# Second-layer expert weights in half-expert parts with two rows a partition: attention and soft mixture of experts on one core

## The chip, the cores and the metric

The kernel runs on 1 core of one Trainium2 chip. The metric is the device time of one execution in microseconds. A core has five engines with queues of their own: TensorE (PE for its matmuls, PEld for its weight loads), VectorE (DVE), ScalarE (ACT), GpSimd (POOL) and SyncE (SP). Transfers are issued from the queues of POOL (these can change the type on the way, here float32 to bfloat16) and of SP (no change of type), and are carried by the same 16 transfer engines.

## The reference

```
q, k, v: (8, 12, 448, 64)         # batch, heads, sequence, head width
scores = 30 * tanh(q @ k.T / sqrt(64) / 30)
attn   = exp(scores - max) / sum
x      = (attn @ v), heads side by side -> (3584, 768)

logits = x @ phi                                  # 3584 x 32: 8 experts x 4 slots
d = softmax of logits over the 3584 tokens;   slot_input = d.T @ x          # 32 x 768
h = relu(slot_input[e] @ w1[e]);   slot_out[e] = h @ w2[e]                  # w1 768x1024, w2 1024x768
c = softmax of logits over the 32 slots;      out = c @ slot_out            # 3584 x 768, float32
```

All eight experts' weights are read once: w1 and w2 are 25 MB each in float32, and no more than 4 rows (slots) pass through each expert.

## The kernel before, in words

**Attention** takes the first 234 us. Heads are worked in pairs, 48 of them; scores of three key tiles at a time go from TensorE (`qk_chunk`, L432) through ScalarE's tanh (`tanh_chunk`, L442) into tiles of six, and then through exp, on ScalarE (`exp_part`, L446) for some tiles and as a polynomial on VectorE (`poly_exp`, L466 to L474, with scratch tiles xf and xp) for the others. TensorE multiplies by v (`pv_mms`, L495), VectorE normalises (L507), and logits and slot sums follow a batch at a time.

**The order is written out by hand** in the string `PROGRAM` (L196 to L243), one letter per step, and each engine does its share in that order. T is a tanh step (0 to 111), Q its scores, E and p the two kinds of exp, A and B the product with v, J and K the transposition of a raw q or k (L389); the transposition of one quad of heads issues the load of the quad after next into the same place (`load`, L278, on POOL's queue). G, N and F are filler matmuls without a use of their own. **M n issues the n-th weight cast** (`wjobs`, L138 to L154), also on POOL's queue.

**The weight casts.** 16 of w1, half an expert each, straight into SBUF (L129). w2 is cut into 64 blocks of 128 rows, ordered so that four experts stand side by side, and four blocks make a part (16 parts, 768 KB each in bfloat16). SBUF has no room for all of w2 during the attention, so most of it is *spilled*: cast from float32 to a bfloat16 copy in DRAM (`load_part`, L136), and read back near the end by SP (`reload`, L162). Six parts are spilled whole, seven in two halves of 384 columns (14 casts), and three are *kept*: cast into SBUF. There are UNITS = 6 places of that size: two *guests* that hold exp tiles until late in the attention, xf, xp, and two free ones. Parts 0 and 1 are kept in the free ones, the last part in the first guest; three reloads go to the other guest, xf and xp. In all 39 casts, M0 to M38.

**The end.** When slot inputs are ready, TensorE does layer 1 (`layer1`, L859; relu on ScalarE and VectorE, L866 and L868), turns h so that its columns lie on partitions (`h_transp`, L876), and does layer 2 (`layer2`, L887): for each part four matmuls side by side in four strips of 32 columns, first all parts for columns 0 to 383 (half 0), then all for the other half. Half 0's result is copied by ScalarE (L935), and while half 1 runs, the first output tiles of half 0 are made (L916) and stored (L904, on SP's queue). The rest of the 3584 x 768 output follows (L963 to L975).

The reloads on SP are issued in the order written at L833: one half part at step O in `PROGRAM` into the place of raw q and k, then whole parts and half-0 pieces, and last the half-1 pieces (L162). SP uses eight semaphores in turn, so a transfer is issued when the eighth before it has landed.

Of the kernel before, what the change touches and what calls it, by code (L numbers as in the profile page):

```python
# [38 lines left out]
def kernel(  # L39
# [29 lines left out]
    KEPT = NFREE + 1  # L69
    UNITS = NFREE + NGU + 2  # L70
    WHOLE = 6
# [43 lines left out]
    blocks = [(i, ft, gg) for i in range(E // 4) for ft in range(NFT) for gg in range(4)]  # L115

    def w2_src(n0, n):

        i, ft, gg = blocks[n0]
        return bass.AP(tensor=moe_w2.tensor,  # L120
                       offset=((4 * i + gg) * F + ft * P) * D,
                       ap=[[D, P], [F * D, n], [1, D]])
# [8 lines left out]
    def load_part(dst, n0, half=None):  # L131
        src = w2_src(n0, 4)
        if half is not None:
            src = bass.AP(tensor=src.tensor, offset=src.offset + half * HD,
                          ap=[[D, P], [F * D, 4], [1, HD]])
        pool.dma_start(out=dst, in_=src)  # L136
# [3 lines left out]
    late = len(w2_parts) - KEPT + NFREE  # L140
    w2_kept = w2_parts[:NFREE] + w2_parts[late:]
    w2_spilled = [(n0, None) for n0 in w2_parts[NFREE:NFREE + WHOLE]]
    w2_spilled += [(n0, half) for half in range(2) for n0 in w2_parts[NFREE + WHOLE:late]]

    dram = ctx.enter_context(tc.tile_pool(name="dram", bufs=1, space=bass.MemoryType.DRAM))
    w2d = {(n0, half): dram.tile([P, 4, D if half is None else HD], BF16, name=f"w2d{n0}_{half}")
           for n0, half in w2_spilled}
    wjobs += [(load_part, w2d[part], *part) for part in w2_spilled]
# [12 lines left out]
    def reload(n, t):  # L161
        sp.dma_start(out=t, in_=w2d[w2_spilled[n]])  # L162
        w2t[w2_spilled[n]] = t

    def reload_raw(n):
        t = rawt[:, 2 - 2 * n:4 - 2 * n, :].rearrange("p n s -> p (n s)")
        reload(WHOLE + n, t[:, 0:4 * HD].rearrange("p (n d) -> p n d", d=HD))

# [34 lines left out]
A5.1 T21 p7.7 t5 B5 m4 M5 E8 u5 p10.0 X1.0 Q22 r5 p10.1 y1 Q23 x1 G19.23 T22.6 p10.2 N1.0 K6.0 m5
T23 Q24 p10.3 X2.1 T24.3 y2 Q25 x2 M6 k6 T25 Q26 p10.4 J6.0 T26.1 L0.1 j6 p10.5 Q27 e0 E11 S0.1
p12.0 A6.0 p10.6 B6 Q28 E9 t6 u6 G23.28 r6 s0 M7 m6 R0.1 p12.1 A7.0 T27 c0 B7 p12.2 t7 u7 K7.1 T28.2
r7 k7 m7 E13 p12.3 A8.0 J7.1 Q29 p10.7 Q30 F9 M8 p12.4 T29 B8 G13.30 j7 T30.4 p12.5 Q31 t8 J8.1 T31
u8 Q32 r8 p12.6 T32.7 Q33 G6.33 m8 T33 Q34 p15.0 K8.0 j8 M9 T34.0 p15.1 N1.1 A9.1 t9 E14 p12.7 B9
p15.2 u9 Q35 k8 N1.0 Q36 p15.3 T35 A10.0 t10 B10 T36.5 r9 p15.4 u10 Q37 m9 M10 T37 Q38 p15.5 J9.1
# [6 lines left out]
m16 W0.1 w0 T51 p24.0 A17.0 J12.1 p22.7 B17 T52.5 t17 u17 p24.1 Q53 G6.53 E25 j12 p24.2 K12.1 Q54
k12 G8.54 r17 p24.3 A18.1 M16 T53 t18 B18 u18 T54.2 r18 m17 Q55 m18 X7.0 T55 p24.4 y7 N1.1 Q56 x7
T56.6 p24.5 A19.0 X8.1 t19 E26 y8 B19 p27.0 u19 Q57 r19 M17 x8 G7.57 p27.1 K13.1 T57 Q58 m19 k13
L2.0 T58.3 p24.6 J13.1 e2 E28 S2.0 j13 p27.2 Q59 p24.7 Q60 A20.1 T59 s2 M18 t20 p27.3 B20 u20 T60.7
Q61 R2.0 r20 T61 c2 Q62 p27.4 K14.0 m20 T62.1 k14 A21.1 p27.5 t21 E30 B21 u21 J14.0 Q63 j14 G10.63
M19 p27.6 X9.0 T63 Q64 y9 x9 T64.4 p27.7 A22.0 B22 p31.0 E29 t22 Q65 r21 p31.1 u22 Q66 m21 G9.66 r22  # L220
p31.2 A23.1 T65 B23 m22 t23 M20 u23 T66.0 r23 A24.0 m23 B24 p31.3 X11.1 E32 t24 y11 Q67 u24 x11 Q68
r24 J15.1 m24 T67 G6.68 j15 p31.4 K15.1 T68.5 A25.0 k15 p31.5 X10.1 M21 E33 B25 y10 t25 u25 Q69 r25
x10 Q70 m25 K16.1 T69 p31.6 L3.0 T70.2 Q71 k16 p34.0 J16.1 T71 Q72 j16 G7.72 p34.1 e3 T72.6 Q73 M22
p31.7 X12.0 y12 T73 p34.2 S3.1 x12 Q74 E35 p34.3 A26.0 Q75 M23 t26 B26 s3 p34.4 u26 R3.1 T74.3 G6.75
r26 c3 m26 A27.1 T75 p34.5 Q76 J17.0 E36 t27 M24 B27 j17 u27 p34.6 K17.0 Q77 G8.77 T76.7 k17 r27
p34.7 A28.0 T77 t28 M25 B28 m27 u28 Q78 r28 E37 p38.0 Q79 A29.1 m28 B29 t29 p38.1 u29 A30.0 B30 r29
T78.4 p38.2 t30 u30 M26 G6.79 r30 m29 T79 Q80 m30 p38.3 A31.1 T80.1 Q81 K18.0 T81 k18 Q82 M27 p38.4
F4 B31 t31 u31 T82.5 J18.0 r31 j18 E39 m31 W1.0 Q83 w1 p38.5 X13.0 X14.1 M28 y13 y14 Q84 x13 T83 x14
N1.0 p38.6 T84.2 Q85 K19.1 J19.0 T85 k19 Q86 M29 j19 L4.1 T86.0 p41.0 Q87 p38.7 e4 E42 S4.1 p41.1
A32.0 s4 p41.2 M30 R4.1 B32 T87 c4 t32 p41.3 X15.1 y15 u32 E40 Q88 Q89 r32 x15 G8.89 m32 M31 p41.4  # L230
K20.0 T88.3 A33.1 k20 B33 p41.5 t33 u33 T89 Q90 J20.0 r33 T90.7 Q91 j20 M32 p41.6 N1.0 T91 Q92 A34.0
m33 E44 F7 p45.0 X16.1 Q93 p41.7 y16 B34 M33 x16 T92.6 t34 u34 p45.1 A35.1 B35 r34 E43 t35 m34 u35
Q94 r35 p45.2 A36.0 t36 m35 F8 M34 p45.3 K21.1 T93 B36 T94.4 k21 Q95 p45.4 u36 J21.1 T95 r36 Q96 j21
G6.96 m36 M35 T96.5 p45.5 Q97 X17.0 T97 y17 Q98 x17 A37.1 T98.1 p48.0 Q99 B37 L5.0 p45.6 M36 T99 t37
u37 e5 r37 E47 m37 K22.0 Q100 p48.1 S5.1 k22 p48.2 J22.0 T100.2 s5 j22 A38.1 E46 p45.7 t38 Q101
p48.3 M37 B38 u38 X18.0 y18 Q102 T101 r38 m38 G12.102 p48.4 T102.0 Q103 x18 A39.1 p48.5 T103 J23.0
t39 B39 u39 E49 j23 r39 p48.6 A40.0 Q104 Q105 m39 t40 T104.3 F10 p48.7 K23.1 B40 T105 k23 u40 O0 r40
M38 R5.1 m40 Q106 E50 c5 A41.0 p52.0 B41 X19.1 p52.1 t41 u41 y19 Q107 x19 T106.4 G7.107 r41 p52.2
A42.1 t42 T107 m41 Q108 p52.3 W2.0 B42 T108.5 u42 Q109 r42 w2 G8.109 E51 m42 Q110 p52.4 X20.1 y20
A43.0 x20 p52.5 L6.1 T109 t43 B43 e6 u43 E53 p52.6 S6.1 Q111 r43 s6 m43 A44.1 E54 p52.7 X21.0 y21  # L240
t44 x21 B44 u44 A45.0 r44 m44 B45 T110.0 t45 u45 A46.1 r45 m45 B46 T111 t46 u46 X22.0 r46 m46 y22
x22 X23.1 y23 x23
# [589 lines left out]

    for n in (0, WHOLE + 2, WHOLE + 3, 1, 2, 3, WHOLE + 1, *range(4, WHOLE), *range(WHOLE + 4, len(w2_spilled))):  # L833
        if n == WHOLE + 1:
            reload_raw(1)
            continue
        shape = [P, 4, HD if n >= WHOLE else D]
        reload(n, unit(shape, BF16, "w2t2") if n < 3 else tl.tile(shape, BF16, name=f"w2t{n}"))
# [5 lines left out]
    def w2_half(n, half):  # L844
        n0 = n - n % 4
        if (n0, half) in w2t:
            return w2t[n0, half][:, n % 4, :]
        t = w2t[n0, None] if (n0, None) in w2t else w2u[w2_kept.index(n0)]
        return t[:, n % 4, half * HD:(half + 1) * HD]
# [34 lines left out]
    def layer2(n0, half):  # L884
        for n in range(n0, n0 + 4):
            i, ft, gg = blocks[n]
            pe.matmul(so_ps[half][32 * gg:32 * gg + NS, :],  # L887
                      hpad[:, 4 * i + gg, ft, :],
                      w2_half(n, half),
                      start=(n0 == 0), stop=(n0 == len(blocks) - 4))  # L890
# [121 lines left out]
```

## Time and profile before

| | |
|---|---|
| median of 3 runs | 281.06 us (280.3 to 282.43) |
| the profiled execution | 281.34 us |
| its span, first to last instruction | 279.4 us |
| mean granted TensorE clock | 0.968 |
| bytes moved by transfers | 69.56 MB, mean 249 GB/s |
| transfers of POOL's queue (q0) | 31840 packets, 35.77 MB, 75.1% of 16 engines' span |
| transfers of SP's queue (q1) | 22880 packets, 32.95 MB, 35.8% |

How to read it: durations come from one profiled execution, whose own time is 281.34 us. Busy rows give the time in which an engine worked; the chain is followed back from the last instruction to whatever released each step; a wait is put down to what ended last before it. Transfer shares can add up to more than 100%, since two transfers can be under way in one engine.

### The profile page before, as it was taken

The numbers are of one execution on the slowest core, as the hardware profiler recorded it, in microseconds if no ns is written. First come the engines' busy times: TensorE is split into PE (matmuls) and PEld (weight loads), VectorE is DVE, ScalarE is ACT, GpSimd is POOL, SyncE is SP. The second block draws the span as 40 slices with busy tenths as digits, with TensorE's granted clock in tenths as the row PEclk, the third lists the DMA queues.
The fourth block names the chain that finished last, engine by engine and source line by source line (L and its number), as shares of the span: only waits on it lengthen the run. The fifth ranks groups of instructions, "written<-read, shape, count | busy, mean of one in ns | idle before, by whom it ended". The sixth has DMA issues, their size and how long they took to land.

```text
span 279.4 us, 9803 instructions
## 1 busy us (share of the span) xinstructions
PE 236.1 (85%) x4151; PEld 150.8 (54%) x4151; DVE 242.2 (87%) x361; ACT 245.1 (88%) x192; POOL 157.6 (56%) x253
## 2 busy tenths in 40 slices
PE   8899889987998988988888898988898998997710
PEld 6435555653565656565665665656566686543300
DVE  3799999998999999999999999999999995337740
ACT  4999999998899999999999999999999997246620
POOL 8489777365586578466885678989725420200000
PEclk9999999997799999999999999999999999999975
DMA  6999999999999999999999999999999999979996
GB/s 181 214 170 220 223 222 223 225 216 223 218 225 229 225 211 227 228 227 218 219 227 228 208 221 219 218 213 216 227 223 245 286 296 405 406 284 378 422 424 268
DMA packets 55051, 69.56 MB, mean 249 GB/s; under 512 B 5984, under 2 KB 45024, under 8 KB 55008
## 3 DMA queue, kind: packets, MB, share of 16 engines
q0 software_dynamic: 31840, 35.77, 75.1%
q1 hardware_dynamic: 22880, 32.95, 35.8%
q8 instruction: 32, 0.52, 0.7%
q10 hardware_dynamic: 288, 0.23, 0.3%
q14 instruction: 11, 0.09, 0.1%
HBM read 93.68 MB, written 21.23 MB: 411 GB/s over the span
## 4 chain that ended last, share of the span: by engine, by line
ACT 44%; DVE 21%; PE 16%; DMA 9%; issue 3%; POOL 2%; DVEq 0%; POOLq 0%; ACTq 0%
ACT ex L442 21%; ACT ex L446 11%; DMA raws<-in_q_dram 6%; ACT exg L442 6%; ACT exg L446 4%; PE pv L495 4%; DVE xq L507 3%; PE sc L432 3%; PE so_ps L887 2%; DMA out_dram<-ob 2%; DVE ex L473 2%; PE hp L859 2%; DVE xf L468 2%; DVE xp L470 2%; DVE xp L472 2%
## 5 line engine op out<-in xcount | busy, mean ns | idle before, releaser
L442 ACT ACTIVATE ex<-sc 128x1344 f16<-128x1344 f32 (+1 forms) x87 | 108.8, 1365 | 2.2 <-PE sc L432 2.1
L432 PE MATMUL sc<-qT,kT 64*128 64x448 bf16 x384 | 68.1, 357 | 8.5 <-ACT ex L442 5.2
L446 ACT ACTIVATE ex<-ex 128x2688 bf16<-128x2688 f16 x27 | 68.4, 2553 | 0.0
L495 PE MATMUL pv<-vbd,ex 128*128 128x65 bf16 (+2 forms) x1041 | 55.5, 201 | 5.4 <-DVE xT L564 1.9
L407 POOL CAST vbd<-vraw 128x384 bf16<-128x384 f32 x46 | 34.1, 742 | 42.4 <-DMA vraw<-in_v_dram 16.5
L495 PEld LDWEIGHTS <-ex 128*128 128x128 bf16 (+1 forms) x1070 | 42.9, 101 | 20.5 <-issue 5.7
L411 POOL CAST vbd<-vraw 64x64 bf16<-64x64 f32 x92 | 48.0, 521 | 2.8
L442 ACT ACTIVATE exg<-sc 128x1344 f16<-128x1344 f32 x26 | 33.2, 1344 | 1.0 <-PE sc L432 1.0
L432 PEld LDWEIGHTS <-kT 64*128 64x128 bf16 x384 | 19.1, 94 | 24.5 <-issue 11.1
L507 DVE TENSOR_TENSOR xq<-pv,rec 128x448 bf16<-128x448 f32 x47 | 28.5, 613 | 0.4
L446 ACT ACTIVATE exg<-exg 128x2688 bf16<-128x2688 f16 x11 | 27.6, 2510 | 0.0
L389 PEld LDWEIGHTS <-raws 128*64 128x64 bf16 x616 | 19.9, 111 | 12.4 <-issue 10.4
L472 DVE TENSOR_TENSOR xp<-xp,xf 128x2688 f16<-128x2688 f16 x17 | 26.4, 1555 | 0.0
L470 DVE TENSOR_TENSOR xp<-xp,xf 128x2688 f16<-128x2688 f16 x17 | 26.2, 1544 | 0.0
L278 POOL DMA_DIRECT2D raws<-in_q_dram x22 | 18.2, 827 | 13.7 <-PE qps L389 8.4
L473 DVE TENSOR_TENSOR ex<-ex,xp 128x2688 uint16<-128x2688 uint16 x15 | 23.1, 1541 | 0.0
L495 PE MATMUL pv<-vbd,exg 128*128 128x65 bf16 (+2 forms) x322 | 20.9, 201 | 2.5 <-DVE xq L507 1.3
L278 POOL DMA_DIRECT2D raws<-in_k_dram x22 | 16.9, 770 | 8.6 <-PE kps L389 8.5
L495 PEld LDWEIGHTS <-exg 128*128 128x128 bf16 (+1 forms) x322 | 14.6, 102 | 8.1 <-issue 4.1
L389 PE MATMUL kps<-ident,raws 128*64 128x128 bf16 x308 | 13.1, 225 | 3.0 <-DVE qT L401 0.9
L471 DVE TENSOR_SCALAR xp<-xp 128x2688 f16<-128x2688 f16 x17 | 15.6, 918 | 0.0
L469 DVE TENSOR_SCALAR xp<-xf 128x2688 f16<-128x2688 uint16 x17 | 14.9, 874 | 0.0
(134 smaller groups left out, 379.0 us busy)
## 6 DMA issues: line engine op xcount, KB each, us to landing
w1b<-in_moe_w_dram POOLq DMA_DIRECT2D x16, 768.0 KB, 12.7
out_dram<-ob SPq DMA_DIRECT2D x8, 768.0 KB, 7.5
vraw<-in_v_dram SPq DMA_DIRECT2D x92, 64.0 KB, 5.7
w2d<-in_moe_w_dram POOLq DMA_DIRECT2D x14, 384.0 KB, 12.0
raws<-in_q_dram POOLq DMA_DIRECT2D x22, 224.0 KB, 10.5
raws<-in_k_dram POOLq DMA_DIRECT2D x22, 224.0 KB, 11.1
w2d_None<-in_moe_w_dram POOLq DMA_DIRECT2D x6, 768.0 KB, 14.5
w2t<-w2d_None SPq DMA_DIRECT2D x6, 768.0 KB, 9.1
```

Source lines behind the costliest of these rows:

```text
L278: pool.dma_start(out=t, in_=quad_ap(nm, Q))
L389: pe.transpose(dst, src[:, h, c * DH:(c + 1) * DH], ident)
L407: pool.tensor_copy(part(t[:, h, :, :], 0, [(CS + 2) * W, 2], [W, CS], [1, DH]), part(raw, 0, [(CS + 1) * DH, 2], [DH, CS], [1, DH]))
L411: pool.tensor_copy(t[r, h, CS + n, 0:DH], raw[r, CS * DH:(CS + 1) * DH])
L432: pe.matmul(sc[:, u, 0:S], qkT["k", Q][r, at:at + P], qkT["q", Q][r, :, n * HP:n * HP + HP], start=(c > 0 or n == 0), stop=(c > 0 or n == 1))
L442: act.activation(exs[j][:, half * CS + u0:half * CS + u1, :].bitcast(F16), sc[:, u0:u1, 0:S], ACT.Tanh, scale=qk_scale / cap)
L446: act.activation(exs[j][:, u0:u1, :], exs[j][:, u0:u1, :].bitcast(F16), ACT.Exp, scale=cap)
L470: lambda: dve.tensor_tensor(p, p, f, op=ALU.mult),
L472: lambda: dve.tensor_tensor(p, p, f, op=ALU.mult),
L473: lambda: dve.tensor_tensor(y, y, p, op=ALU.add),
L495: pe.matmul(out_, exs[j][:, u, q0:q0 + (HP if tail else P)], v_, start=(c == 0 and g == gs[0] < NF), stop=(c >= NT - 2), skip_group_check= ...
L507: dve.tensor_tensor(xq[Q][:, h, s0:s1, :], pv[:, 0:s1 - s0, 0:DH], recs.pop(pr).to_broadcast([P, s1 - s0, DH]), op=ALU.mult)
```

## The change

- A part of w2 is now half of one expert, four blocks of 128 rows (`blocks` is (expert, block)). Partition p holds rows 2p and 2p+1 of a stretch of 256 rows, so one descriptor reads two rows (6 KB in float32) and writes 3 KB in bfloat16, where it read one row or half a row before. `h_transp` takes the columns of h in the same interleaved order.
- Four parts are kept: 0 and 1 in the free units, and 2 and 3 in the two guests, cast late (M30 and M31). The other twelve are spilled whole.
- Parts 4 and 5 are read back in pieces of two blocks (one of each into the place of raw q and k), parts 6 and 7 into xf and xp, 8 to 14 whole, and part 15 in two halves of columns at the end.
- There are 32 casts, M0 to M31, at new places in `PROGRAM`: M6, for instance, stood before J6.0 and now stands behind it; M27, the last spill, stands at T94 where M35, the last one before, stood at T96.
- A few fillers are changed (ten places, by some matmuls each).

```
-    KEPT = NFREE + 1
+    KEPT = NFREE + NGU
-    WHOLE = 6
+    WHOLE = 9
...
-    blocks = [(i, ft, gg) for i in range(E // 4) for ft in range(NFT) for gg in range(4)]
+    blocks = [(e, ft) for e in range(E) for ft in range(NFT)]
+    def w2_src(n0):
+        e, ft = blocks[n0]
+        return bass.AP(tensor=moe_w2.tensor, offset=(e * F + ft * P) * D,
+                       ap=[[2 * D, P], [2 * P * D, 2], [1, 2 * D]])
...
+    def load_part(dst, n0):
+        pool.dma_start(out=dst.rearrange("p (a n) d -> p a (n d)", n=2), in_=w2_src(n0))
...
+    w2_kept = w2_parts[:KEPT]
+    split = len(w2_parts) - WHOLE - 1
+    w2_spilled = w2_parts[KEPT:]
...
+    def reload(n0, b0, b1, h0, h1, t):
+        sp.dma_start(out=t, in_=w2d[n0][:, b0:b1, h0 * HD:h1 * HD])
...
     def reload_raw(n):
         t = rawt[:, 2 - 2 * n:4 - 2 * n, :].rearrange("p n s -> p (n s)")
+        reload(w2_parts[split - 2 + n], 2 * n, 2 * n + 2, 0, 2,
+               t[:, 0:2 * D].rearrange("p (n d) -> p n d", d=D))
...
-x1 G19.23 T22.6 p10.2 N1.0 K6.0 m5 T23 Q24 p10.3 X2.1 T24.3 y2 Q25 x2 M6 k6 T25 Q26 p10.4 J6.0
+x1 G16.23 T22.6 p10.2 K6.0 m5 T23 M5 Q24 p10.3 X2.1 T24.3 y2 Q25 x2 k6 T25 Q26 p10.4 J6.0 ... B6 M6
...
+    def reload_tl(n, b0=0, b1=4, h0=0, h1=2):
+        shape = [P, b1 - b0, (h1 - h0) * HD]
+        n0 = w2_parts[n]
+        t = unit(shape, BF16, "w2t2") if split <= n < split + 2 else tl.tile(shape, BF16, name=f"w2t{n}_{b0}_{h0}")
+        reload(n0, b0, b1, h0, h1, t)
+
+    reload_tl(split - 2, 2, 4)
+    reload_tl(split - 1, 0, 2)
+    reload_tl(split)
+    reload_tl(split + 1)
+    reload_raw(1)
+    for n in range(split + 2, split + WHOLE):
+        reload_tl(n)
+    for half in range(2):
+        reload_tl(split + WHOLE, 0, 4, half, half + 1)
...
-            pe.matmul(src[:, ft - t0, :, :], hbs[i][:, ft * P:(ft + 1) * P], own,
+            pe.matmul(src[:, ft - t0, :, :], hbs[i].rearrange("p (q f r) -> p q f r", r=2, f=P)[:, ft // 2, :, ft % 2], own,
...
-            i, ft, gg = blocks[n]
-            pe.matmul(so_ps[half][32 * gg:32 * gg + NS, :],
-                      hpad[:, 4 * i + gg, ft, :],
+            e, ft = blocks[n]
+            pe.matmul(so_ps[half][32 * (n - n0):32 * (n - n0) + NS, :],
+                      hpad[:, e, ft, :],
                       w2_half(n, half),
```

More of the change, by code (lines that the diff above doesn't have):

```diff
@@ L129, in load_w1 @@
         pool.dma_start(out=w1b[e][:, js, :], in_=w1r[:, e, js, :])
[L131 to L136, printed above, removed]
+    def load_part(dst, n0):
+        pool.dma_start(out=dst.rearrange("p (a n) d -> p a (n d)", n=2), in_=w2_src(n0))
     wjobs = [(load_w1, e, jh) for e in range(E) for jh in range(2)]
     w2_parts = list(range(0, len(blocks), 4))
[L140 to L143, printed above, removed]
+    w2_kept = w2_parts[:KEPT]
+    split = len(w2_parts) - WHOLE - 1
+    w2_spilled = w2_parts[KEPT:]
     dram = ctx.enter_context(tc.tile_pool(name="dram", bufs=1, space=bass.MemoryType.DRAM))
-    w2d = {(n0, half): dram.tile([P, 4, D if half is None else HD], BF16, name=f"w2d{n0}_{half}")
-           for n0, half in w2_spilled}
-    wjobs += [(load_part, w2d[part], *part) for part in w2_spilled]
+    w2d = {n0: dram.tile([P, 4, D], BF16, name=f"w2d{n0}") for n0 in w2_spilled}
+    wjobs += [(load_part, w2d[n0], n0) for n0 in w2d]
     def load_kept(n):
@@ L159 @@
     w2t = {}
-    def reload(n, t):
-        sp.dma_start(out=t, in_=w2d[w2_spilled[n]])
-        w2t[w2_spilled[n]] = t
+    def reload(n0, b0, b1, h0, h1, t):
+        sp.dma_start(out=t, in_=w2d[n0][:, b0:b1, h0 * HD:h1 * HD])
+        for n in range(b0, b1):
+            for half in range(h0, h1):
+                w2t[n0 + n, half] = t[:, n - b0, (half - h0) * HD:(half - h0 + 1) * HD]
     def reload_raw(n):
         t = rawt[:, 2 - 2 * n:4 - 2 * n, :].rearrange("p n s -> p (n s)")
-        reload(WHOLE + n, t[:, 0:4 * HD].rearrange("p (n d) -> p n d", d=HD))
+        reload(w2_parts[split - 2 + n], 2 * n, 2 * n + 2, 0, 2,
+               t[:, 0:2 * D].rearrange("p (n d) -> p n d", d=D))
     att = ExitStack()
@@ L203 @@
[L203 to L208, printed above, removed]
@@ L215 @@
[L215 to L220, printed above, removed]
@@ L221 @@
[L221 to L235, printed above, removed]
@@ new lines @@
+B31 t31 u31 T82.5 J18.0 r31 M23 j18 E39 m31 W1.0 Q83 w1 p38.5 N1.1 X13.0 X14.1 y13 y14 Q84 x13 T83
+x14 N1.0 p38.6 T84.2 Q85 K19.1 J19.0 T85 k19 Q86 j19 L4.1 M24 T86.0 p41.0 Q87 p38.7 e4 E42 S4.1
+p41.1 A32.0 s4 p41.2 R4.1 B32 T87 c4 t32 p41.3 X15.1 y15 u32 E40 Q88 Q89 r32 x15 G8.89 m32 M25 p41.4
+K20.0 T88.3 A33.1 k20 B33 p41.5 t33 u33 T89 Q90 J20.0 r33 T90.7 Q91 j20 p41.6 N1.0 T91 Q92 A34.0 m33
+E44 F7 p45.0 X16.1 M26 Q93 p41.7 y16 B34 x16 T92.6 t34 u34 p45.1 A35.1 B35 r34 E43 t35 m34 u35 Q94
@@ new lines @@
+r35 p45.2 A36.0 t36 m35 F8 p45.3 K21.1 T93 B36 M27 T94.4 k21 Q95 p45.4 u36 J21.1 T95 r36 Q96 j21
+G6.96 m36 T96.5 p45.5 Q97 X17.0 T97 y17 Q98 x17 A37.1 T98.1 p48.0 Q99 B37 L5.0 p45.6 T99 M28 t37 u37
+e5 r37 E47 m37 K22.0 Q100 p48.1 S5.1 k22 p48.2 J22.0 T100.2 s5 j22 A38.1 E46 p45.7 t38 Q101 p48.3
+B38 u38 X18.0 M29 y18 Q102 T101 r38 m38 G10.102 p48.4 T102.0 Q103 x18 A39.1 p48.5 T103 J23.0 t39 B39
+u39 E49 j23 r39 p48.6 A40.0 Q104 Q105 m39 t40 T104.3 F10 p48.7 K23.1 B40 T105 k23 u40 O0 r40 M30
+R5.1 m40 Q106 E50 c5 A41.0 M31 p52.0 B41 X19.1 p52.1 t41 u41 y19 Q107 x19 T106.4 G7.107 r41 p52.2
@@ L831 @@
     tl = ctx.enter_context(tc.tile_pool(name="tl", bufs=1, reuse_waits="tile"))
[L833 to L838, printed above, removed]
+    def reload_tl(n, b0=0, b1=4, h0=0, h1=2):
[12 more added lines that the diff above has]
+        reload_tl(split + WHOLE, 0, 4, half, half + 1)
     hpad = tl.tile([P, E, NFT, NS], BF16, name="hpad")
@@ L844, in w2_half @@
     def w2_half(n, half):
[L845 to L849, printed above, removed]
+        if (n, half) in w2t:
+            return w2t[n, half]
+        return w2u[n // 4][:, n % 4, half * HD:(half + 1) * HD]
     hbs = {}
```

51 lines of the change are left out of this document (31 added, 20 removed).

## The prediction

> **What bounds the kernel now.** I read the page first: busy time, granted clock, transfers, the chain.
>
> ```profile
> span 279.4 us, 9803 instructions
> ...
> PE 236.1 (85%) x4151; PEld 150.8 (54%) x4151; DVE 242.2 (87%) x361; ACT 245.1 (88%) x192; POOL 157.6 (56%) x253
> ...
> PEclk9999999997799999999999999999999999999975
> DMA  6999999999999999999999999999999999979996
> ...
> ACT ex L442 21%; ACT ex L446 11%; DMA raws<-in_q_dram 6%; ACT exg L442 6%; ACT exg L446 4%; PE pv L495 4%; DVE xq L507 3%; PE sc L432 3%; PE so_ps L887 2%; DMA out_dram<-ob 2%; DVE ex L473 2%; PE hp L859 2%; DVE xf L468 2%; DVE xp L470 2%; DVE xp L472 2%
> ```
>
> The chain is ScalarE's tanh (L442) and exp (L446), with one foreign piece of note, a load of q. The transfer engines are full almost everywhere, and the granted clock dips once. The windows view takes the attention apart; columns are PE, PEld, DVE, ACT and POOL busy, clock, DMA share, GB/s.
>
> ```profile
> 8.50:60.00 51.50, 45.81 (x747) 27.08 (x744) 49.76 (x68) 51.43 (x37) 34.95 (x53) 1.00 1.15 214
> ...
> 63.60:67.03 3.43, 1.95 (x36) 1.21 (x34) 2.24 (x5) 2.94 (x3) 0.33 (x1) 1.00 1.14 230
> 67.03:73.85 6.82, 6.19 (x62) 3.45 (x59) 6.82 (x10) 6.09 (x4) 4.33 (x6) 0.50 1.18 215
> ...
> 100.00:234.40 134.40, 119.76 (x2327) 81.26 (x2324) 131.14 (x198) 134.37 (x97) 89.74 (x135) 1.00 1.18 234
> ```
>
> ScalarE works 51.43 of 51.50 us and 134.37 of 134.40: there nothing but less ScalarE work can gain, and the change takes none away. It idles around 64 to 76 us alone. The waits of ScalarE from 8.5 to 234, those of TensorE from 62 to 76, and the chain from 48 to 84 tell why.
>
> ```profile
> ACT exg L442 <- PE sc L432: 1.0, 1, 1.0
> ACT ex L442 <- PE sc L432: 1.0, 3, 0.6
> ```
> ```profile
> PE qps L389 <- DMA raws<-in_q_dram: 1.0, 1, 1.0
> ```
> ```profile
> 52.59 13.55 DMA raws<-in_q_dram
> ...
> 66.19 0.58 PE qps L389 x14
> ...
> 67.51 1.30 ACT exg L442
> ```
>
> The q load was issued at 52.59 and landed at 66.14. TensorE stood 1.0 us for it, then ScalarE 1.0 for TensorE. The window with that gap had TensorE busy 1.95 of 3.43 us, and the clock was 0.50 for the next 6.82 us, in which ScalarE lost 1.0 more. Sum 2.0 us, one cause.
>
> After 234 us the end is serial; the chain from 243 to 270 and ScalarE's timeline:
>
> ```profile
> 244.79 2.88 PE so_ps L887 x68
> ...
> 250.70 1.12 PE so_ps L887 x24
> ...
> 255.02 3.81 DMA out_dram<-obh
> ```
> ```profile
> 247.06 0.48 ACT L935 CAST so<-so_ps 128x384 bf16<-128x384 f32 x1 [2.69 <-PE so_ps L887]
> ```
>
> Half 0 of layer 2 is finished at 247.06, half 1 at 251.82, and from 255 the output transfers bound.
>
> **The change, part by part.** *Order of the casts.* 39 become 32: the spills go from 6 whole and 14 half parts to 12 whole, the kept from 3 to 4. In the program the cast M6 now stands behind J6.0, which issues the q load of 52.59. GpSimd's timeline, and the landings of that k load (48.98) and cast (49.72):
>
> ```profile
> 46.22 1.10 POOL L129 DMA_DIRECT2D w1b<-in_moe_w_dram  x1
> ...
> 48.98 0.74 POOL L278 DMA_DIRECT2D raws<-in_k_dram  x1
> 49.72 0.76 POOL L129 DMA_DIRECT2D w1b<-in_moe_w_dram  x1
> 52.59 0.74 POOL L278 DMA_DIRECT2D raws<-in_q_dram  x1 [2.12 <-PE qps L389]
> ```
> ```profile
> DMA to landing us min/median/max: 11.2/11.2/11.2
> ```
> ```profile
> DMA to landing us min/median/max: 14.7/14.7/14.7
> ```
>
> The queue lands in order: k at 48.98 + 11.2 = 60.2, the cast at 49.72 + 14.7 = 64.4, q at 66.1. The cast costs q 4.2 us. One fewer ahead puts q at 61.9, 3.3 us before TensorE wants it (66.19 less the 1.0 it waited). The wait and, with it, the clock dip go: **-2.0 us**, between 0 (another load late instead) and -2.0; ScalarE has no more idle time to give. Later casts are issued later or at the same place against k and q, so I see none next in line, but I keep it as a rival.
>
> *Fewer issues.* Seven fewer at GpSimd's own prices:
>
> ```profile
> L136 POOL DMA_DIRECT2D w2d<-in_moe_w_dram x14 | 12.3, 878 | 0.6 <-issue 0.6
> L136 POOL DMA_DIRECT2D w2u<-in_moe_w_dram x3 | 3.3, 1085 | 0.1
> ```
>
> 7 x 0.88 = 6 us off GpSimd, busy 56%: nothing on the path. M31, a second kept cast behind M30, puts 1.1 us ahead of three V casts, which wait for their V transfers anyway; SP's V loads stand behind those casts with equal cover. If that cover is gone it costs 1.1 us once. M30 and M31 wait for their guests, last filled by T92 and T90 of 111 and long read by then.
>
> *3-KB packets.* They make casts shorter in a stage that ScalarE bounds: nothing, beyond the queue above.
>
> *TensorE's fillers (G, N, F)* move by a few matmuls, under ScalarE: nothing. The interleaved columns of hb make 16 weight loads strided; a contiguous one is 96 ns in the L876 rows, and no row has a strided one: 0 to 16 x 0.1 = 1.5 us. I take 0, since each is followed by waits for weights (next).
>
> *The reloads, the cost.* SP's timeline, and the last reload with its landing:
>
> ```profile
> 224.94 2.39 SPq L162 DMA_DIRECT2D w2t<-w2d_None  x3
> 227.37 0.43 SPq L162 DMA_DIRECT2D raws<-w2d  x1
> 227.91 2.45 SPq L162 DMA_DIRECT2D w2t<-w2d_None  x2
> 230.45 11.79 SPq L162 DMA_DIRECT2D w2t<-w2d  x10
> 248.61 9.37 SPq L904 DMA_DIRECT2D out_dram<-obh  x13
> ```
> ```profile
> L162 SPq DMA_DIRECT2D w2t<-w2d x1: 319/319/319, 241.9 to 241.9; - x1
> ...
> DMA to landing us min/median/max: 7.7/7.7/7.7
> ```
>
> On SP only the stores stand behind the reloads. Today half 0's weights come first and seven half-1 pieces last, ending at 241.9 + 7.7 = 249.6. Now parts 8 to 14 come whole, and part 15 in two halves at the end: half 0 needs all but the very last transfer. From 224.94, when xf comes free, the bytes are the same: before 5 x 768 + 11 x 384 = 8064 KB, after 9 x 768 + 3 x 384 = 8064 KB. Before 224.94 there are 768 KB less to move (part 2 is cast into a guest unit instead), worth 768/413 = 1.9 us at most. One cast more runs beside the reloads, which eats most of it; I take 0.6 of it as gained, with ends 0 and 1.9. Against that, part 15's halves are cut from a whole tile, 512 rows of 768 bytes instead of 128 of 3 KB. Transfers of the SP queue, in a window of reloads alone (232 to 245, which also gives 413 GB/s) and in one of V loads (20 to 200):
>
> ```profile
> DMA packets 1565, 5.37 MB, mean 413 GB/s; under 512 B 172, under 2 KB 172, under 8 KB 1562
> ...
> q1 hardware_dynamic: 1562, 5.33, 101.2%
> ```
> ```profile
> q1 hardware_dynamic: 12091, 8.68, 19.5%
> ```
>
> 13 us x 16 x 1.012 / 1562 is 135 ns for 3.4 KB; 180 x 16 x 0.195 / 12091 is 46 ns for 0.72 KB. So each of the halves takes 32 x 0.049 = 1.55 us instead of 0.95, both 1.2 more. The last lands at 249.6 + 1.2 - 0.6 = 250.2, part 15's half 0 at 248.7, and half 0 ends at 248.9 instead of 247.06: **+1.9**, ends 0.5 and 3.0. The Trainium skill, "DMA: Bandwidth & Descriptors", section "Specifications", holds 512 bytes enough for line rate; by that the two halves would cost nothing extra and the sum would be about 0.8 us lower, while the rows above disagree (46 ns for 0.72 KB).
>
> What of it reaches the end: the outputs shift by 1.9, but no reload is left among them, where now 249.6 - 248.6 = 1.0 us of reloads shares the engines with the first stores. Part of that returns, since the early stores are paced by TensorE and not by the transfers:
>
> ```profile
> 246.00:249.00 3.00, 3.00 (x60) 1.31 (x52) 0.78 (x2) 1.06 (x2) 0.00 (x0) 1.00 0.61 243
> 249.00:252.00 3.00, 3.00 (x46) 1.02 (x42) 1.85 (x4) 1.75 (x3) 0.00 (x0) 1.00 0.77 280
> 251.30:254.80 3.50, 2.29 (x22) 0.81 (x13) 2.47 (x5) 1.63 (x4) 0.00 (x0) 1.00 0.94 347
> ```
>
> DMA share 0.61 and 0.77. I take 0.6 of the 1.0 back: **+1.3** at the end, ends 0 and +2.7.
>
> **Sum.** The profiled execution took 281.34 us. 281.34 - 2.0 + 1.3 = 280.6; the median of the runs is 281.06, 0.28 below the profiled one, well inside their spread (280.3 to 282.43), so I do not correct for it. About 1% is what a measurement can tell from no change.
>
> **Rivals.** *No price at the end* (0.2): the casts finish early, reloads gain the full 1.9 us, and half 0 waits 0.5: 281.34 - 2.0 + 0 = 279.3. For it: fewer casts are in the queue by 200 us. Against it: the units xf and xp come free no earlier.
>
> *Half clock in layer 2* (0.2), the slower side: TensorE, waiting some 1.9 us for parts 14 and 15, falls below what keeps its clock. The row at 63.60 (busy 1.95 of 3.43, 57%) was followed by 6.82 us at 0.50; that at 251.30 (2.29 of 3.50, 65%) was not. A wait of 1.9 wholly inside such a stretch leaves about 45 to 55%, split over two about 70%. It decides from a wait of some 1.4 us in one stretch. Half 1 and the early output matmuls (247.06 to 251.82) would then lose half of 6.8 us, 3.4, of which some 0.4 is hidden by stores: 280.6 + 3.0 = 283.6. The Trainium skill, "TensorE: Matmul & The Clock Gate", section "Why this matters for your kernels", says that gaps up to about 3 us do no harm; by that this rival falls away and 280.6 stands. The trace disagrees, with its dip after a 1.0-us wait.
>
> *The order does not help* (0.15): another k or q load is late, or TensorE is stalled elsewhere, so the 2.0 stays while the end pays: 281.34 + 1.3 = 282.6.
>
> **How the numbers follow.** My forecast has 0.45, its own range is 279.3 to 282.0 (281.34 - 2.0 with 0 to 2.7 at the end). All cases together: 278.9 to 284.0, leaving out 0.1 on each side. Faster by over 1% needs 278.25 or less, 1.1 below the no-price rival: 0.07. Slower by over 1% needs 283.87: the upper half of the half-clock rival, alone or with a late load: 0.14. Within 1%: 0.79.
>
> **What would show it.** Right: no TensorE wait for in_q_dram and clock full to the end of attention, with the last exps some 2 us earlier; SP's last reload landing about 0.6 us later against that end; a TensorE wait on w2t before the last eight half-0 matmuls; first store 1.9 us later against layer 1. Wrong: a new TensorE wait on a k or q load, or a 0.50 stretch after 245, or layer 2 without a wait.

## The result, and the profile after

The changed kernel takes 287.96 us (median of 6 runs, 286.91 to 291.07) against 281.09 us: a ratio of 1.0254, 95% interval 1.0202 to 1.0307. It is slower; the prediction was 280.6 us and its range ended at 284.0. The profiled execution took 288.14 us. The page after, in the lines that answer to those shown before, with the rows of the two transfer queues (packets, MB, share of 16 engines):

```profile
span 286.1 us, 9812 instructions
...
PE 238.2 (83%) x4163; PEld 151.4 (53%) x4163; DVE 241.4 (84%) x361; ACT 245.1 (86%) x192; POOL 154.9 (54%) x246
...
PEclk9999999998699999999999999999999999979975
DMA  6999999999999999999999997999999999929995
...
q0 software_dynamic: 24048, 35.77, 71.0%
q1 hardware_dynamic: 22928, 32.16, 33.3%
```

No engine but TensorE works longer than before (ScalarE 245.1 us both times); TensorE works 238.2 us instead of 236.1, over 10.2 us of half clock instead of 6.8. The added time is idle: a hole in the DMA row near the end, and a second dip of the clock there. The windows show both dips and what stood ahead of each:

```profile
66.50:69.90 3.40, 2.21 (x29) 1.12 (x27) 3.40 (x6) 3.40 (x4) 2.90 (x5) 1.00 1.14 207
69.90:76.70 6.80, 6.74 (x71) 4.08 (x70) 6.80 (x9) 5.44 (x4) 4.61 (x5) 0.50 1.13 195
...
247.40:250.80 3.40, 0.69 (x8) 0.20 (x8) 0.00 (x0) 0.00 (x0) 0.00 (x0) 1.00 0.85 298
250.80:254.20 3.40, 3.28 (x31) 0.99 (x31) 0.62 (x1) 1.06 (x2) 0.00 (x0) 0.50 0.04 12
```

From 247.40 to 250.80 TensorE works 0.69 us of 3.40 and nothing else computes. Its timeline there names the reason in the brackets:

```profile
245.87 1.31 PE L890 MATMUL so_ps<-w2t,hpad 128*32 128x384 bf16 x28
247.90 0.35 PE L890 MATMUL so_ps<-w2t,hpad 128*32 128x384 bf16 x4 [0.72 <-DMA w2t<-w2d]
249.92 0.35 PE L890 MATMUL so_ps<-w2t,hpad 128*32 128x384 bf16 x4 [1.67 <-DMA w2t<-w2d]
250.92 0.51 PE L890 MATMUL so_ps<-w2t,hpad 128*32 128x384 bf16 x4 [0.65 <-DMA w2t<-w2d]
```

Each group of four matmuls is one part, and parts 13, 14 and 15 each wait for their reload: 3.0 us. Then the clock halves and the matmuls of half 1 run at half speed. The copies of the two halves (ScalarE, VectorE) give the sizes:

```profile
251.48 0.48 ACT L938 CAST so<-so_ps 128x384 bf16<-128x384 f32 x1 [6.30 <-PE so_ps L890]
```
```profile
257.55 0.56 DVE L946 CAST so<-so_ps 128x384 bf16<-128x384 f32 x1 [0.65 <-PE so_ps L890]
```

Layer 1 starts at 238.80 (before 238.06), half 0 ends 12.68 us later (before 9.00), half 1 6.07 us after it (before 4.78). The last output lands at 284.91 instead of 278.49. Of these 6.42 us, 0.74 are there when layer 1 starts, 3.68 come in half 0, 1.29 in half 1, and 0.71 behind it.

### The profile page after: what moved, and what is told of

It is laid out like the page before. It is cut to its first block, busy times and chain, and to the rows that moved or that the text cites. A ratio compares the mean times of both kernels' runs of the same rounds, so it can differ in the third digit from the quotient of the medians.

```text
span 286.1 us, 9812 instructions
## 1 busy us (share of the span) xinstructions
PE 238.2 (83%) x4163; PEld 151.4 (53%) x4163; DVE 241.4 (84%) x361; ACT 245.1 (86%) x192; POOL 154.9 (54%) x246
## 3 DMA queue, kind: packets, MB, share of 16 engines
q0 software_dynamic: 24048, 35.77, 71.0%
## 4 chain that ended last, share of the span: by engine, by line
ACT 49%; PE 18%; DMA 14%; DVE 10%; issue 3%; POOL 1%; DVEq 0%; SPq 0%; ACTq 0%; POOLq 0%
ACT ex L438 22%; ACT ex L442 11%; ACT exg L438 8%; ACT exg L442 7%; DMA raws<-in_q_dram 5%; PE pv L491 5%; DMA w2t<-w2d 4%; PE sc L428 3%; DMA out_dram<-ob 2%; DMA vraw<-in_v_dram 2%; PE so_ps L890 2%; DVE ex L469 2%; PE op L919 1%; DVE xq L503 1%; DVE xp L468 1%
## 5 line engine op out<-in xcount | busy, mean ns | idle before, releaser
L403 POOL CAST vbd<-vraw 128x384 bf16<-128x384 f32 x46 | 38.2, 830 | 51.1 <-issue 18.9
L407 POOL CAST vbd<-vraw 64x64 bf16<-64x64 f32 x92 | 47.2, 513 | 2.8
L438 ACT ACTIVATE exg<-sc 128x1344 f16<-128x1344 f32 x26 | 33.9, 1395 | 0.0
L274 POOL DMA_DIRECT2D raws<-in_q_dram x22 | 16.9, 767 | 11.5 <-PE qps L385 9.6
L397 DVE COPY qT<-qps 128x896 bf16<-128x896 bf16 x23 | 14.1, 615 | 1.7 <-PE qps L385 1.6
L467 DVE TENSOR_SCALAR xp<-xp 128x2688 f16<-128x2688 f16 x17 | 15.0, 883 | 0.0
```

The source lines that it names most:

```text
L274: pool.dma_start(out=t, in_=quad_ap(nm, Q))
L403: pool.tensor_copy(part(t[:, h, :, :], 0, [(CS + 2) * W, 2], [W, CS], [1, DH]), part(raw, 0, [(CS + 1) * DH, 2], [DH, CS], [1, DH]))
L407: pool.tensor_copy(t[r, h, CS + n, 0:DH], raw[r, CS * DH:(CS + 1) * DH])
L438: act.activation(exs[j][:, half * CS + u0:half * CS + u1, :].bitcast(F16), sc[:, u0:u1, 0:S], ACT.Tanh, scale=qk_scale / cap)
```

## The experiments

The table has, for each profiled execution, when layer 1 starts, and how long after that half 0 ends (the copy of so[0] starts), half 1 ends, and the last reload lands; then TensorE's wait for w2t; then when the last output has landed, again counted from layer 1's start; and the ratio to the kernel before with its 95% interval. The ratio comes from several runs and includes the attention; the other columns are one execution each. In the profiled executions of m6_moved, before_mixed and halves_no_both layer 1 starts three to five us late; of them, no time ahead of layer 1's start is compared, except m6_moved's near 62 us, since its clock was full until 172.

| kernel | layer 1 | half 0 | half 1 | reloads | wait | outputs | ratio |
|---|---|---|---|---|---|---|---|
| before | 238.06 | 9.00 | 13.78 | 11.59 | 0 | 40.43 | 1 |
| after | 238.80 | 12.68 | 18.75 | 13.09 | 3.0 | 46.11 | 1.0254 (1.0202–1.0307) |
| halves_first | 237.65 | 8.85 | 16.99 | 16.39 | 2.6 | 43.35 | 1.0052 (1.0009–1.0095) |
| fill_wait | 236.51 | 12.55 | 17.33 | 13.09 | 0.5 | 44.31 | 1.0130 (1.0094–1.0166) |
| before_mixed | 243.35 | 10.65 | 15.43 | 11.82 | 1.5 | 42.41 | 1.0096 (1.0046–1.0147) |
| hybrid_fill | 236.79 | 10.16 | 14.95 | 14.51 | 0 | 41.45 | 1.0067 (1.0013–1.0120) |
| no_m31 | 236.72 | 12.54 | 17.32 | 13.12 | 3.1 | 44.97 | 1.0038 (0.9983–1.0094) |
| no_m30_m31 | 239.41 | 9.02 | 13.81 | 9.00 | 0 | 41.59 | 1.0110 (1.0020–1.0200) |
| halves_no_m31 | 237.38 | 8.85 | 13.63 | 12.04 | 0 | 40.54 | 1.0018 (0.9979–1.0058) |
| halves_no_both | 242.48 | 8.85 | 13.64 | 13.05 | 0 | 40.77 | 0.9952 (0.9906–0.9998) |

**halves_first: the order undone.** Parts 8 to 15 are reloaded as halves, all halves 0 first:

```diff
-    for n in range(split + 2, split + WHOLE):
-        reload_tl(n)
     for half in range(2):
-        reload_tl(split + WHOLE, 0, 4, half, half + 1)
+        for n in range(split + 2, split + WHOLE + 1):
+            reload_tl(n, 0, 4, half, half + 1)
```

> The changed kernel with the reloads of parts 8 to 15 cut in halves of columns, all first halves ahead of all second ones (as the kernel before had it for parts 8 to 14). Theory A, the order of the reloads: half 0's weights then land by about 244 to 245, before layer 2 wants them, so the 3.1 us of waits for w2t go, and with them the half clock in layer 2 (1.3 us) and the thinner start of the stores (0.7 us): 287.96 - 5.1 = 282.9 us, first store near 249.5. Theory B, the sum of the reloads: they end too late in any order, the last landing still at about 252 to 253, so that half 1 waits where half 0 did: 285.5 to 287.

Measured: 282.69 us. Half 0 waits for nothing and ends at 8.85. The wait reappears in half 1, followed by the same half clock:

```profile
PE so_ps L889 <- DMA w2t<-w2d: 2.6, 3, 1.7
```
```profile
250.40:253.80 3.40, 1.04 (x20) 0.30 (x9) 0.24 (x1) 0.42 (x1) 0.00 (x0) 1.00 1.05 371
253.80:260.60 6.80, 5.61 (x19) 1.73 (x19) 4.26 (x7) 3.31 (x6) 0.00 (x0) 0.50 0.82 306
```

In half 1 it is cheaper: outputs of half 0 are stored meanwhile, and the transfer engines' share is 1.05 and 0.82 in these rows, where the changed kernel has 0.04 behind its wait. Undoing the order takes 0.0202 off the ratio, 5.7 us of 7.1. The two profiled executions show 2.8 of it behind layer 1's start and 1.2 ahead of it. But the reloads as a whole are late in this order too, at 16.39. Some 1.7 us of that are the price of the halves: there are sixteen, and they land 1.06 us apart here (fifteen from 237.25 to 252.04), where those of the kernel before, with 3-KB rows, land 0.95 apart.

**fill_wait: the clock held.** Spare matmuls ahead of the waits of half 0:

```diff
+    WAITS = {52: 2, 56: 6, 60: 3}
...
+        if n0 in WAITS:
+            spare(WAITS[n0], 0)
         layer2(n0, 0)
```

> The changed kernel with 2, 6 and 3 filler matmuls in front of the last three parts of half 0, where TensorE waits for weights. If the half clock after that wait costs 1.3 us by itself (half 1 took 6.1 us instead of 4.8), the clock stays full, half 1 takes about 4.8 us and the time is 286.5. If the wait alone counts, and the output transfers hide the rest, it stays at 287.9.

Measured: 284.64 us. Half 0 ends as late as before the edit (12.55), so the weights still pace it, but TensorE stays busy and half 1 takes 4.78 us again:

```profile
243.40:246.80 3.40, 3.18 (x47) 1.48 (x40) 0.02 (x1) 0.00 (x0) 0.00 (x0) 1.00 1.02 397
246.80:250.20 3.40, 3.11 (x40) 1.11 (x38) 0.24 (x1) 0.56 (x2) 0.00 (x0) 1.00 0.39 131
250.20:253.60 3.40, 3.40 (x54) 1.12 (x46) 2.23 (x4) 2.25 (x4) 0.00 (x0) 1.00 0.40 143
```

From so[0] to the last output it is 31.76 us, against 33.43 in the changed kernel: the half clock costs 1.7 us by this pair. (The executions of all kernels whose clock stays full there take 31.2 to 32.6, so by them it is 0.9 to 2.2.) The rest of the gain is an attention stage that ended sooner (236.51), with no dip of the clock.

**m6_moved: the cast alone.** In the kernel before, M6 goes from ahead of k6 to behind B6.

> The kernel before with one cast, M6, moved behind the q load that TensorE waited for. By the prediction's first step the wait of 1.0 us and the half clock behind it both go: 281.09 - 2.0 = 279.1. Its rival: with the q load early TensorE only runs ahead and waits for VectorE a little later, the clock dips in the next stretch all the same, and the time stays at 281.

Measured: 280.9 us, ratio 1.0001 (0.9980 to 1.0022). The q load lands at 61.83 and its wait is gone, but another, of 1.3 us, is next in line:

```profile
PE pv L495 <- DVE xq L507: 1.3, 1, 1.3
```

**fill_68 and before_fill: stronger fillers near 68 us.** G6.33 becomes G12.33 and G7.34 is added behind K8.0, in the changed kernel and in the kernel before.

> The changed kernel with 13 more small filler matmuls between 67 and 70 us, in TensorE's gaps ahead of its clock dip. If the dip (0.50 from 69.9 to 76.7) is what ScalarE's 2.1 us of waits at 74 and 77 us come from, it goes, the exps end 2 us earlier, and the time is 286.0. If those waits come from VectorE being late, they stay: 287.9.

> The kernel before with the stronger fillers around T33 and T34 (12 in place of 6 short matmuls, and 7 more behind K8.0), nothing else. The prediction priced the late q load and the half clock behind it at 2.0 us. If the half clock is 1.0 of it and fillers hold it: 280 to 280.4. If the stage from 64 to 76 us is paced by VectorE whether or not the clock drops: no change, 280.9 to 281.3. If the fillers delay score matmuls that ScalarE waits for: above 281.5.

Measured: 287.94 us, ratio 1.0246 (1.0174 to 1.0317), and 280.79 us, ratio 1.0009 (0.9965 to 1.0053). The dip near 70 is gone in both profiled executions; the median does not move. fill_68's execution was late from elsewhere (full clock came only at 16.9 us, and layer 1 started at 241.37), so it tells little; before_fill says that this dip is no fixed cost of the kernel's runs. The granted clock of the runs says so too: of the 67 runs of the kernel before that enter the ratios here, 48 have a mean clock of 0.977 or more and a median of 280.6 us, and 19 a lower one and 282.8. The profiled execution before had 0.968.

**before_mixed: the order alone.** The kernel before, with its last ten half transfers in the order of the change:

```diff
-    for n in (0, WHOLE + 2, WHOLE + 3, 1, 2, 3, WHOLE + 1, *range(4, WHOLE), *range(WHOLE + 4, len(w2_spilled))):
+    for n in (0, WHOLE + 2, WHOLE + 3, 1, 2, 3, WHOLE + 1, 4, 5, 13, 14, 15, 16, 10, 17, 11, 18, 12, 19):
```

> The kernel before with one edit: the last reloads in the order of the changed kernel (the halves 1 of the first four half-loaded parts come before the last halves 0, and only the very last transfer, part 15's half 1, stands behind half 0's needs). Bytes, casts and row sizes stay as before. Theory A (the order of the reloads alone makes half 0 of layer 2 late): a wait on w2t of 1.5 to 2.5 us before the last half-0 matmuls, so[0] at 249 instead of 247.06, first store at 250.5; 282.5 to 284, the upper end if the clock drops in half 1. Rival B (the order costs nothing; the later end of the last reload, from later casts, is the loss): no wait above 0.7 us, 280.5 to 281.5.

Measured: ratio 1.0096 (1.0046 to 1.0147), some 2.7 us. The wait is where theory A put it, and half 0 ends 1.65 us later against layer 1's start:

```profile
PE so_ps L887 <- DMA w2t<-w2d: 1.5, 1, 1.5
```

The last output lands 2.0 us later against layer 1's start. The order costs by itself; but this is less than half of the loss.

**no_m31, m29_early, no_m30_m31: the late casts.** One kernel drops the token M31, one moves M29 ahead of u38, one drops M30 and M31; where a cast is dropped, w2_half reads an earlier part's tile.

> The changed kernel without the last cast M31 (part 3 of the second layer's weights is not loaded; layer 2 takes part 2's weights for it, so its output is not the reference's). All reloads and their order stay. Theory A (order and row size): the last reload still lands about 13 us after layer 1's start (after: 13.1), half 0 still waits about 3 us, 287 to 288. Rival B (the casts that are still in flight when the reloads start share the engines with them): the last reload lands 11 to 11.5 us after layer 1's start (before: 11.6), half 0 waits 1.2 to 1.7, and the time is 284.5 to 286.

> The changed kernel with the cast M29 moved in front of the V cast u38 on GpSimd, which waited 4.5 us for TensorE: M29 is issued at about 202.5 instead of 208.25. Theory A: M29 to M31 land up to 3 us earlier, the last reload at most 0.5 us earlier against layer 1's start, half 0's wait stays near 3 us, 287 to 288. Rival B (late casts delay the reloads): the last reload 1 to 1.5 us earlier against layer 1's start, 285.5 to 286.5.

> The changed kernel without the two last casts M30 and M31 (parts 2 and 3 of the second layer's weights are not loaded, and layer 2 takes part 1's for them, so its output is not the reference's). The kernel without M31 alone came out some 5 us faster by its times, while the wait for w2t in its profiled execution was as long as in the changed kernel (3.1 us). Theory B (each late cast takes engine time from the V loads and reloads): without both, the last reload lands 11 us or less after layer 1's start, half 0's wait is under 1.5 us, 280 to 281.5. Theory A (only order and row size set the wait): last reload 13 us after layer 1's start, wait 3 us, 283 to 285 by an undisturbed attention stage alone.

Measured: no_m31 ratio 1.0038 (0.9983 to 1.0094), m29_early 1.0208 (1.0130 to 1.0286), no_m30_m31 1.0110 (1.0020 to 1.0200). M29's place hardly matters (reloads 12.50 instead of 13.09, and a ratio whose interval overlaps the changed kernel's). For M31 time and profile disagree: its ratio is 0.0216 lower, some 6 us, yet its profiled execution has the old wait. That execution, 284.89 us, is the longest of the seven runs behind the ratio (from 280.69), so it need not speak for the others. GpSimd's timeline and the windows show what stood in for the cast there:

```profile
214.53 0.90 POOL L131 DMA_DIRECT2D w2u<-in_moe_w_dram  x1
222.62 1.16 POOL L403 CAST vbd<-vraw 128x384 bf16<-128x384 f32 x1 [7.18 <-DMA vraw<-in_v_dram]
```
```profile
220.00:225.00 5.00, 4.83 (x120) 3.70 (x120) 4.74 (x5) 5.00 (x4) 2.38 (x2) 1.00 0.64 207
225.00:230.00 5.00, 4.90 (x101) 3.73 (x100) 4.31 (x11) 5.00 (x4) 2.99 (x8) 1.00 0.68 232
```

In this execution the last V load was issued 0.68 us behind M30 (215.21 against 214.53) and landed with it, at 222.46; the V casts that empty the raw tiles waited, SP waited 4.5 us for it and 3.0 for a V cast behind it, so that the third reload was issued at 225.60, and the transfer engines stood a third idle. In halves_no_m31 the same load was issued 0.55 us ahead of M30 and landed at 219.27. Without both casts the reloads end 9.00 us after layer 1's start and half 0 ends at 9.02, without a wait. That its ratio is not better than no_m31's goes with an attention stage that ended 2.7 us later in its profiled execution. The trace shows why: TensorE waited 2.49 us for a q load, until 210.50, the clock was 0.50 from 211.67, and ScalarE waited 2.52 us. The page has the wait in its row of the q transpositions:

```profile
L385 PE MATMUL qps<-ident,raws 128*64 128x128 bf16 x308 | 12.7, 221 | 2.6 <-DMA raws<-in_q_dram 2.5
```

All four of its runs have a granted clock of 0.970 to 0.972 as that one has. Why this q load is late stands in the next section.

**halves_no_m31, halves_no_both: both causes taken away.** halves_first, without M31, and without M30 and M31.

> halves_first (the changed kernel with parts 8 to 15 in halves, all halves 0 first) without the cast M31 (part 3 is not loaded, layer 2 takes part 2's weights for it, so its output is not the reference's). If the order of the reloads and the late casts are two separate causes, the waits for w2t that halves_first had in half 1 (2.6 us) go as well, the last reload lands 1.5 to 2 us sooner against layer 1's start than its 16.4, and the time is 280.5 to 281.3. If the order alone is the cause, nothing changes against halves_first: 282 to 283.

> halves_first without the casts M30 and M31 (parts 2 and 3 are not loaded, layer 2 takes part 1's for them, so its output is not the reference's). Two causes: no wait for w2t in either half, half 0 done 8.8 to 9.1 us after layer 1's start, half 1 4.8 us behind it, 280 to 281, which is then what attention and the stores alone set. One cause: 282 to 283.

Measured: 1.0018 (0.9979 to 1.0058) and 0.9952 (0.9906 to 0.9998). No wait for weights is left, and the reloads of halves_no_m31 end 4.35 us sooner than those of halves_first for one cast less. From layer 1's start to the last output it is 40.54 and 40.77 us, against 40.43 before and 46.11 in the changed kernel: the order and the late casts account for the whole loss behind layer 1's start. These two kernels also cast one and two parts fewer than the kernel before. A kernel that casts all sixteen parts, M31 among the early ones, was not run; that it is the lateness of the cast which costs, and not the work in it, rests on halves_first, which casts the same sixteen parts as the kernel before, reloads in its order, and still waits; the 1.7 us of its short rows are in that too. So it is shown that M31 costs, and argued that it does so by standing late.

**hybrid_fill, fill_both, best_try: can it be mended with all work done?** hybrid_fill has parts 11 to 15 in halves and four spare matmuls; fill_both is fill_wait with fill_68's fillers; best_try is hybrid_fill with M29 ahead of u38 and those fillers.

> The changed kernel with the reloads of parts 11 to 15 in halves, halves 0 first (parts 8 to 10 stay whole), and 4 spare matmuls of 512 columns in the last waits of half 0. Half 0 then needs all but five half-transfers, which half 1 takes up at the pace of its own 4.8 us. Theory A: so[0] about 9.5 us after layer 1 starts (before 9.0, after 12.7), no wait above 0.7 us in half 1, clock full after 245, last reload about 14 us after layer 1's start; 281 to 283. Rival B: the wait moves into half 1 and the end stays at 285 or above.

> The changed kernel with the spare matmuls of fill_wait before parts 13, 14 and 15 in half 0, and the stronger fillers of fill_68 around T33 and T34. Theory: holding the clock in layer 2 gives 2 to 3 us against the changed kernel, and holding it at 70 us about 1 us more where the changed kernel drops it: 283.5 to 284.5. Rival: what made fill_wait faster was an attention stage without a drop by chance, and filling both gives 286 to 287.

> hybrid_fill (parts 11 to 15 in halves, halves 0 first, spare matmuls in half 0) with M29 in front of u38 and with the stronger fillers around T33 and T34. If the scatter of hybrid_fill (281.2 to 285.2) comes from clock drops around 70 and 210 us, this one gives 281 to 282 throughout, the same as before; if from the casts that land beside the V loads, it stays at 282 to 284. Neither theory expects it below 280.5, since VectorE and ScalarE pace attention and the transfers pace the rest.

Measured: 1.0067 (1.0013 to 1.0120), 1.0126 (1.0017 to 1.0235), 1.0045 (1.0005 to 1.0086). The layer-2 stalls can be hidden, and best_try's runs scatter less (281.46 to 284.00 where hybrid_fill's go to 285.18); but half 0 still ends 1.2 to 1.5 us later than before in both (10.16 and 10.49 us after layer 1's start). In part that is the spare matmuls themselves: part 15's half 0 had landed at 246.02 and 245.85, and its matmuls, behind spare ones, start at 246.55 and 247.46. None of the three beats the kernel before.

## Why the prediction was wrong

*The sum failed in the term for the reloads*: +1.3 us at the end, with +1.9 in half 0. Measured are +3.68 in half 0 and, with its consequences, 5.7 behind the start of layer 1, 4.4 more than the term. Most of the rest is the first step: layer 1 starts 0.74 us later in the profiled execution, and not 2.0 sooner. In the reloads the cast was priced too low and the halves too high, and a rival came true that had been kept apart from a larger wait.

*"768 KB less to move, 1.9 us; one cast more runs beside the reloads, which eats most of it."* The cast eats more than all of it. The page's queue rows price it: 35.77 MB take 71.0% of 286.1 us on queue q0, so the 0.786 MB of one part take 4.5 us of all 16 engines, against 1.9 us for a reload of the same bytes. This is the mean of the queue, with its q and k loads; the trace's 3-KB packets alone, which are the parts of w2, take 251 ns each, and the 256 of one part 4.0 us. The 4.35 us between halves_first and halves_no_m31 are close to that price, in one pair of executions; without M30 and M31 the reloads end 4.09 sooner for both casts, and no_m31's profile shows no gain, for the reason above. I had counted a cast's issue (1.1 us of GpSimd) and a reload's bytes, and never a cast's time on the engines. What it competed with is in GpSimd's timeline of the changed kernel, with the landings of M30 and M31 behind it:

```profile
206.95 0.88 POOL L403 CAST vbd<-vraw 128x384 bf16<-128x384 f32 x1 [4.53 <-PE pv L491]
...
208.25 0.92 POOL L131 DMA_DIRECT2D w2u<-in_moe_w_dram  x1
...
216.86 1.79 POOL L131 DMA_DIRECT2D w2u<-in_moe_w_dram  x2
```
```profile
DMA to landing us min/median/max: 8.3/10.7/13.1
```

The two are issued at 216.86 and 217.75 and land at 225.16 and 230.83, among the reloads. At 229.71 the changed kernel had landed two of its reloads (768 KB) since 214; the kernel before had landed four by 229.11 (1920 KB). That is 1152 KB less, of which 768 need no reload; so it was 384 KB behind, 0.95 us at 413 GB/s. One cast more and 768 KB of reloads less make 4.0 - 1.9 = 2.1 us; the reloads end 1.5 us later against layer 1, where I had them 0.6 later. I also left M29's queue out: it stands behind u38, which waited 4.53 us for TensorE. By m29_early this cost 0.6 us of the reloads at most.

*"The halves of part 15 take 1.55 us instead of 0.95."* Too dear. They land 1.0 us apart in the changed kernel (249.88, 250.88, 251.89). A stretch of halves_first with halves only, beside the same stretch of the changed kernel, nearly all whole rows:

```profile
DMA packets 3693, 2.77 MB, mean 346 GB/s; under 512 B 111, under 2 KB 3692, under 8 KB 3692
```
```profile
DMA packets 981, 3.26 MB, mean 408 GB/s; under 512 B 71, under 2 KB 508, under 8 KB 978
```

By these packets 768-byte rows move at 0.85 of the rate of whole rows, which are 6 KB here; by the landings of halves_first, 1.06 us for a half, it is 0.9 of the 413 GB/s. My 46 ns came from V loads, which share the engines with casts. The rule of the Trainium skill that I weighed against it ("DMA: Bandwidth & Descriptors", "Specifications": 512 bytes are enough for line rate) was much nearer than my row, though not exact.

*The rival, half clock in layer 2, came true.* I gave it 0.2 and 3.0 us. It was put at a wait of 1.4 us in one stretch, and the stretch had 2.7 us idle. fill_wait prices it at 1.7, so its price was too high, and its time of 283.6 too low because the wait was larger. Its condition was right; I took the wait for small because the reload term was too small. A range that joined this rival to a larger wait, one leading to the other, and to the late load, would have come near: 281.34 + 2.7 + 3.0 = 287.0. The Trainium skill's rule ("TensorE: Matmul & The Clock Gate", "Why this matters for your kernels": no idle gaps above about 3 us, so as to avoid drops) was not enough here: 247.40 to 250.80 has no gap over 1.67 us, and the clock dropped.

*The first step, −2.0 for the late q load, was right about that load and gave nothing.* The load lands early:

```profile
L274 POOL DMA_DIRECT2D raws<-in_q_dram x1: 736/736/736, 52.5 to 52.5; - x1
...
DMA to landing us min/median/max: 8.7/8.7/8.7
```

That is 61.2 (I had 61.9), and the wait for it is gone. Next in line there was no load, as I feared, but VectorE: TensorE waits 1.3 us for xq, the clock drops at 69.90, and ScalarE waits more than the 2.0 us that it did before. The wait alone does not decide it: no_m31, hybrid_fill and best_try have the same 1.3 us and no dip. In no_m31's execution ScalarE waits for nothing to speak of. The changed kernel and no_m31, ScalarE's waits in attention:

```profile
ACT ex L438 <- PE sc L701: 1.2, 1, 1.2
ACT ex L438 <- PE sc L428: 1.1, 2, 0.9
```
```profile
ACT ex L438 <- PE sc L428: 0.2, 1, 0.2
```

There layer 1 starts at 236.72, 2.1 us sooner than in the changed kernel. So the gain exists, execution by execution; it isn't a fixed term of the sum, and m6_moved, with a ratio of 1.0001, shows that the median holds none of it. I priced one profiled execution's dip as if every run had it.

And the load that I feared came, further on. I saw no cast newly placed ahead of a q load; but M27, a whole part, is issued between the k load of 194.64 and the q load of 198.66, where the kernel before issued its last two loads without a cast between them. M27 lands at 209.53 and the q load behind it at 210.88, 12.2 us after its issue (before 9.9). TensorE's waits in the changed kernel show it, at 210.92, as long as the one that went away at 66.19:

```profile
PE qps L385 <- DMA raws<-in_q_dram: 1.0, 1, 1.0
```

Eight of the twelve profiled executions with this order of casts wait here, for 0.26 to 2.49 us, and none of the four with the old order does. In the changed kernel ScalarE did not feel the 1.0 us; in no_m30_m31 and m29_early waits of 2.5 and 2.1 us were followed by half clock, and ScalarE lost 2.5 us in each. So the rival "another k or q load is late" came true in part: one late q load was exchanged for another. How much of the median is due to it no run shows, since none was made with M27 elsewhere.

*Costed at nothing, and nothing seen against it:* fewer issues and fillers. *Costed at nothing and right:* hb's columns. Their 16 weight loads take 97 ns each (before 96), and from layer 1's start to half 0's end it is 9.02 us where no weight is waited for (no_m30_m31), against 9.00 before, and ScalarE's work is the same. The 3-KB packets did make the casts cheaper, 203 us of queue q0 for the same bytes against 75.1% of 279.4 = 210, under ScalarE.

## What to carry to other kernels

Price a transfer by its queue's share of the engines, not by its bytes: a converting load can take more than twice a plain one, and one that is kept late costs the loads behind it more than the reload that it saves. When pieces are merged, ask which is the last piece that the first consumer needs: the same bytes in another order cost 2.7 us by themselves here. When casts change places, look at every load that is issued behind one, and not only at the one to be helped. A drop of the clock needs a wait of TensorE, though not every wait brings one, so the range must contain both together; and a dip that one profile shows is to be found in other executions before it is taken as a gain.

## What the runs showed of the hardware

The granted clock is less regular than my two rows suggested. Windows of about 3.4 us with TensorE busy for 0.69, 1.04 and 2.21 us were followed by 0.50; one of no_m31, with 1.68 us busy and layer 2's waits of 3.1 us in and ahead of it, was not:

```profile
243.40:246.80 3.40, 1.98 (x44) 1.05 (x37) 0.22 (x1) 0.00 (x0) 0.00 (x0) 1.00 1.01 398
246.80:250.20 3.40, 1.68 (x26) 0.69 (x25) 0.03 (x1) 0.48 (x1) 0.00 (x0) 1.00 0.49 165
250.20:253.60 3.40, 3.40 (x51) 1.24 (x54) 2.44 (x4) 2.33 (x4) 0.00 (x0) 1.00 0.32 113
```

In each of the sixteen executions the changes of the clock stand whole multiples of 3.41 us apart (in the changed kernel's 69.89, 76.72, 250.80 and 254.21: 2, 51 and 1 of them). Counted by this grid, over all kernels here, full-clock stretches with TensorE busy for 1.50 us or less were followed by 0.50 in all of 21 cases, those with 2.25 or more in none of 1149, and those between in 5 of 42. (On this grid no_m31's two, from 243.61 to 250.44, have 1.77 and 1.92 and are between.) What decides in that band was not settled.

How long the last V load takes goes with its place against M30. Issued 0.25 to 1.7 us ahead of M30, it landed after 4.1 to 4.3 us (three executions); 0.3 to 0.5 behind it, after 4.9 to 5.6 (three); 0.7 to 1.3 behind it, after 6.3 to 7.3 (four), and the third reload was then issued at 225.6 or later instead of at 221.4 to 223.5. Two executions without M30 took 5.4 and 5.6, so the place explains the extremes and not all of it. In three of the four late ones M31 filled the transfer engines meanwhile; in no_m31 they stood a third idle for ten microseconds.
